# Inner fifth products in three more units of a gated feed-forward pass, with its sums placed anew

## The chip, the cores and the metric

The kernel runs on one core of a Trainium2 chip. The metric is the time of one execution on the device, in microseconds (us); lower is better.

## The reference

A pre-norm block of two parts, for 2048 tokens of width 1024, inputs and output in bfloat16:

```
h  = x + A(layernorm(x))       # linear attention: wqkv, 32 heads, phi(t) = (t+1 if t>0 else exp(t)) + 1e-6, wo
h2 = h + B(layernorm(h))
B(x) = (relu(x @ W_gate) * (x @ W_up)) @ W_down     # 1024 -> 3584 -> 1024
```

The change lies in B. It does not touch the attention part.

## The kernel before, in words

**Products by seven instead of eight.** A matrix product is cut into 2 x 2 blocks and done as seven block products P1 to P7 instead of eight (Strassen's scheme, in Winograd's form). It needs sums of blocks of the activations (`Ssum`, four arrays S1 to S4) and of the weights (`Tring`, four arrays T1 to T4 for each unit). The sums of the results are made partly in PSUM: a finished P1 is copied by ScalarE into the bank where the next product goes on adding (the forks `fk1`, `fk2`), and P5 is kept in SBUF (`s5`) and added at the evacuations c22 and c12.

**An inner step.** One of the block products can itself be done by seven smaller ones: 14 matmuls of 256 columns instead of 8 of 512. For P1 these are R1 to R7, done during the unit before (line 1725, `inner1`, says for which units). For P5 they are M1 to M7, at the start of the unit and between its other products (line 1722, `M0`, lists the units of pass 0; pass 1 does it in all). The inner P5 needs four sums xs of S1, once for a pass (`x_inner`, in `xs5`), and three instructions g5 for each unit on its T1 (`w_inner`, from T1 to `g5`); the sum `s5a` on VectorE takes the place of two copies by ScalarE, and small copies M5c, M1c, M6c and M4c come in. The inner P1 likewise needs three instructions g1 (`w_inner1`) on the raw weights and a sum Ra in PSUM.

**Two passes, units and a down pass.** The feed-forward part works on 1024 tokens at a time (pass 0 and pass 1). A pass has 14 units (`ffn_unit`, line 1728): even units compute the gate, with relu, odd ones the up projection, with the multiplication by the gate, both for the same four tiles of 128 of the 3584 columns; unit n uses ring slots of raw weights W (three units deep) and of T. The results `hh` stay in SBUF. Then the down pass multiplies them by W_down, again by seven products (pi = 0 to 6), most of which are themselves done by seven (`level2`: M1, M7, M6, M2, M5, M4, M3, each of 28 matmuls of 256 columns, with one weight load of 448 KB); in pass 0 products 0 and 2 are plain (`direct`: five chunks of weights). They use the four PSUM banks `XB` or `YB`. Loaded weights pass through a ring of 7 slots in pass 0 and 9 in pass 1, in the order of the list `WLIST`.

**Sums of sums.** The down pass needs sums of `hh`: D1 and D3 (`hh_pair`, two tiles at a time, done by VectorE in odd units), D2 and D4, and from them the inner sums sg3 to sg7. It also needs sums of W_down. VectorE makes those of the first level from raw weights (WT, `wd_pair`) in even units and of the second (WL, `wl_sums`) in odd ones; GpSimd makes some of the second level (WM and half of WL in pass 0; WY, `y_wsums`, in pass 1). All are stored in DRAM and loaded again in the down pass. A GpSimd sum waits for the matmul that was issued last when it was put into the program; its place in a unit is a call of `run(mid, n)`.

**LayerNorm of pass 1** (LN) is spread over the units of pass 0: for each of eight tiles a mean and a square on ScalarE, each followed by small steps of GpSimd on 128x1 (`_v`, `_v2`, `_r`, `lnn`), and a normalization. It goes to DRAM and comes back transposed (T5d, a DMA). Four of the tiles come back early into `hnE`, and ScalarE copies them (`hnc`, `early_c`) into `hnT`, when pass 0 no longer reads it. In this kernel `hnE` lies in RE, on the place of `xs5` and `g5`, so it is filled from unit 11 on.

**What sets the order.** The order of each engine's work is written out by hand. An instruction is appended to its engine's program when the Python code reaches it, and each engine, and the SP queue that issues most DMAs, runs its program in that order. In `ffn_unit` lists of further work are put into fixed places: `pre` at the start, `wina` after the first products, `winb` ahead of P7, then c22, `lnb` and `winc`, later c12 and `tail`, then P4. `lna` comes early in a unit without the inner P5 and after c22 in one of pass 0 with it. In the down pass `at(pi, ci, ...)` puts work behind part ci of product pi. Waits follow from `_Buf` objects: a reader waits for the last writer, a writer for all readers, and `over` or `claim` name other buffers on the same memory.

Almost all matmuls have line 904 in the profile, ScalarE's copies 909, most VectorE work of a unit 1776, and g1, g5 line 1688, T 1644 and 1649, D1 and D3 1665 and 1668, sg 1987, D2, D4 and the sums of the down pass 2051, WM 881, GpSimd's WL 871, WY 806.

Of the kernel before, what the change touches and what calls it, by code (L numbers as in the profile page):

```python
# [132 lines left out]
def bass_sequential_preLN__linear_attn_block__glu_gated_reglu__prompt_kernel(  # L133
# [71 lines left out]
    with es:  # L205
# [80 lines left out]
        hnE = RE[:, 4 * D:8 * D].rearrange("p (t a c) -> p t a c", t=STB, c=P)  # L286
# [52 lines left out]
        xn = RXH[:, 0:NXN * D].rearrange("p (a b) -> p a b", a=NXN)  # L339
        TWo_x = RXH[:, 0:KH * D].bitcast(f16).rearrange("p (j k c) -> p j k c", j=2, k=KH)  # L340
# [240 lines left out]
        for b_ in B_D1:  # L581
            b_.over = B_xn + B_TWo[0::2] + B_hs + hp_x
# [14 lines left out]
        for b_ in B_hnE:  # L597
            b_.over = B_o + B_oT[0:NOE]
        for b_ in B_hnE:
            b_.over = b_.over + B_xs5 + flat(B_g5)  # L600
        for b_ in B_xs5 + flat(B_g5):
            b_.over = B_o + B_oT[0:NOE]
        for b_ in B_V:
            b_.over = B_hnE
# [103 lines left out]
        ORDER = [list(range(7)), [0, 2, 1, 3, 4, 5, 6]]  # L708
# [952 lines left out]

        def hh_pair(q):
            f1, f2, f3 = 2 * q, 2 * q + 1, 2 * q + 4
            t0, t1 = slice(0, SBW), slice(SBW, 2 * SBW)
            PL.add("dve", lambda e: e.tensor_tensor(out=D1[:, q:q + 2, :], in0=hh[:, f1:f3:2, t1],
                                                    in1=hh[:, f2:f3:2, t1], op=ALU.add),
                   reads=[B_hh[f][1] for f in range(f1, f3)], writes=B_D1[q:q + 2], name="D1_%d" % q)
            PL.add("dve", lambda e: e.tensor_tensor(out=hh16[:, f1:f3:2, t1], in0=hh[:, f1:f3:2, t0],
                                                    in1=hh[:, f1:f3:2, t1], op=ALU.subtract),
                   reads=[B_hh[f][0] for f in (f1, f1 + 2)], writes=[B_hh[f][1] for f in (f1, f1 + 2)],  # L1670
                   name="D3_%d" % q)
# [56 lines left out]
        def ffn_unit(ps_, n, pre, wina, winb, mid=(), lna=(), lnb=(), tail=(), tail2=(), winc=()):  # L1728
# [211 lines left out]
            go(lnb)  # L1940
# [3 lines left out]
            go(winc)  # L1944
# [10 lines left out]
            evac5(1, 0, BC_, c12, B_c12, "c12")  # L1955
            go(tail)
# [76 lines left out]
        def down_pass(ps_, fill):  # L2033
# [128 lines left out]
            def d2(a, b):  # L2162
                tt(D2[:, a:b, :], D1[:, a:b, :], hh[:, 2 * a:2 * b:2, 0:SBW],
                   B_D1[a:b] + [B_hh[2 * q][0] for q in range(a, b)], [B_D2], "D2", op=ALU.subtract)

# [6 lines left out]
            def direct(pi, bk, act_ops, start, evac):  # L2172
                af, ab = act_ops
                for ci, (q0, q1) in enumerate(WCH):
                    def go(ci=ci, q0=q0, q1=q1):
                        ws = wd_slot(wd_use[0])
                        wd_use[0] += 1
                        w = wdring[ws]

                        def d_mm(q, j):  # L2180
                            mm(bank(bk[j]), af(q, j), w[:, (q - q0) * NW:(q - q0 + 1) * NW], start and q == 0,
                               q == NPAIR - 1, [ab(q), B_wd[ws]], B_bank[bk[j]], "d%d_%d_%d" % (pi, ps_, q), skip=True)

                        if q1 == NPAIR:
                            for j in range(STB):
                                for q in range(q0, q1):
                                    d_mm(q, j)
                            load_wd_next()
                            for j in range(STB):
                                evac(j)  # L2190
                        else:
                            for q in range(q0, q1):
                                for j in range(STB):
                                    d_mm(q, j)
                            load_wd_next()
                    units.append(((pi, ci), go))
# [89 lines left out]
            claim([B_D2], B_S)  # L2286
# [9 lines left out]
            for i in range(4):  # L2296
                at(1, 2 + i if not last else (2, 3, 4, 5)[i], sg7[i])
            if not last:
                at(0, 0, lambda: d2(0, NH), lambda: d2(NH, NPAIR))
                at(0, 1, sg6[0])  # L2300
                at(0, 2, *sg6[1:3])
                at(0, 3, sg6[3])
                for i in range(4):
                    at(2, 1 + i, sg5[i])
                claim(B_sgg, B_w[0:4])
                at(2, 2, lambda: d4(0, NH))
                for i in range(4):
                    at(2, 1 + i, sg4[i])
                at(3, 0, lambda: d4(NH, NPAIR))
            else:  # L2310
# [9 lines left out]
                at(0, 6, lambda: d2(0, NH))  # L2320
                at(2, 0, lambda: d2(NH, NPAIR))
# [330 lines left out]
        for p_ in range(NPASS):  # L2652
            done = []
            for q in range(NPAIR):
# [9 lines left out]
                if q > 1 and q % 2:  # L2664
                    wina.append(lambda q=q: hh_pair(q - 3))
                if p_ == 0:
                    raw, lna, lnb, tail = [], [], [], []
                    if q > 0 and ln_q:
                        for t in done:
                            early.append(t)  # L2670
                        f_, t0 = ln_q.pop(0)
                        lna.append(f_)
                        f_, t1 = ln_q.pop(0)
                        lnb.append(f_)
                        done = [t for t in (t0, t1) if t is not None and t < STB]
                    winc = []
                    for _ in range(2 if q == NPAIR - 1 else 1):
                        if q > 10 and early:
                            early_t(early.pop(0))
                    if q % 2 == 0:  # L2680
                        wds = wd_pair(q)
                        (tail if q == 0 else wina).extend(wds[0:2])
                        (tail if q == 0 or q in M0 else winb).append(wds[2])
                        wls, raw, nxt_raw, raw_l = wl_sums(q // 2)
                    else:
                        wina += wls
                        raw = raw_l
                        nxt_raw()
                        if q == NPAIR - 1:
                            for _ in range(4):  # L2690
# [11 lines left out]
                    ffn_unit(0, q, pre, wina, winb, raw, lna, lnb, tail, winc=winc)  # L2702
# [5 lines left out]
                if q == 0:  # L2708
# [6 lines left out]
                    wys = [f_ for m in range(NM) for f_ in y_wsums(m)]  # L2715
# [23 lines left out]
                if q == NPAIR - 1:  # L2739
# [3 lines left out]
                    for i in range(NWX):  # L2743
                        claim([B_wd[NWS + i]], [B_w[i]])
                        load_wd_next()
            for f_ in late21:
                f_()
            late21.clear()
            hh_pair(NPAIR - 2)
# [4 lines left out]
            else:  # L2754
                claim(B_V, B_xs5 + flat(B_g5))
# [4 lines left out]
            if p_ + 1 < NPASS:  # L2760
                late = [(lambda t=t: early_c(t), (0, t)) for t in range(STB)]
                late += [(lambda t=t: late_t(t), ((0, 1), (0, 3), (2, 0), (2, 1))[t - STB]) for t in range(STB, TPP)]
# [9 lines left out]
                late += [(nxt_s, (3, 1))] + [(ss[i], ((3, 3), (3, 5), (6, 0), (6, 2))[i]) for i in range(4)]  # L2772
# [71 lines left out]
```

## Time and profile before

| what | value |
|---|---|
| median of 3 runs | 710.98 us (710.78 to 712.07) |
| the profiled execution | 711.03 us |
| its span | 709.3 us |
| granted TensorE clock | 0.999 of full speed |
| units of pass 0 | 222.6 to 389.1 of the span |
| down pass of pass 0 | 389.1 to 466.8 |
| units of pass 1 | 466.8 to 631.0 |
| down pass of pass 1 | 631.0 to 706.4 |

The page counts an engine as busy while any of its instructions runs, so a pipelined TensorE appears nearly full; pauses are found from the starts of its matmuls and from the chain of work, which names the instruction that released each step. In a row of stretches, `11.69 (x69)` is the busy time and the number of instructions in it; the last three numbers are the granted clock, the DMA engines' busy share and GB/s. The digits of the 40 slices of the span, each 17.7 us, show where VectorE is full:

```profile
DVE  7988867899899899999998787887989888989996
ACT  4887666764863687778785411146666667651010
POOL 3221100114893334243522001321111110000331
```

### The profile page before, as it was taken

To read this page: it belongs to the slowest core of one execution; us is meant where nothing else is said; L and a number is where in the kernel's file an instruction comes from. 1 tells how busy PE (TensorE), PEld (TensorE's weight loads), DVE (VectorE), ACT (ScalarE), POOL (GpSimd) and SP (SyncE) were. 2 spreads that over 40 slices of the span, in tenths; PEclk is the share of its full clock that TensorE was granted. 3 is DMA by queue.
4 is the path that set the end of the run, shared out by engine and by line. 5 is a ranking of instruction groups with operands and counts; after the bars stand their busy time and mean duration, and the time that the engine had idled before them with its cause. 6 is when DMAs were issued, how large, how long until landed. Compare 5 with 4: busy or idle time off the path is not lost.

```text
span 709.3 us, 13488 instructions
## 1 busy us (share of the span) xinstructions
PE 704.0 (99%) x5101; PEld 398.3 (56%) x5101; DVE 612.4 (86%) x970; ACT 409.6 (58%) x743; POOL 179.5 (25%) x246
## 2 busy tenths in 40 slices
PE   9999999999999999999999999999999999999998
PEld 4444444444444455555554658865555555568887
DVE  7988867899899899999998787887989888989996
ACT  4887666764863687778785411146666667651010
POOL 3221100114893334243522001321111110000331
PEclk9999999999999999999999999999999999999999
DMA  9852244014999795968899999998465644268996
GB/s 304 255 123 61 39 133 161 29 31 97 231 208 285 233 345 170 304 215 252 271 292 290 310 243 320 315 243 239 133 190 156 193 147 125 87 236 312 345 283 184
DMA packets 170385, 148.80 MB, mean 210 GB/s; under 512 B 54352, under 2 KB 146896, under 8 KB 170320
## 3 DMA queue, kind: packets, MB, share of 16 engines
q1 hardware_dynamic: 165328, 143.35, 67.2%
q0 software_dynamic: 4032, 3.67, 3.5%
q8 instruction: 40, 0.66, 0.4%
q10 hardware_dynamic: 960, 0.92, 0.4%
q14 instruction: 25, 0.20, 0.1%
HBM read 101.97 MB, written 33.88 MB: 192 GB/s over the span
## 4 chain that ended last, share of the span: by engine, by line
PE 93%; DVE 3%; DMA 2%; issue 1%; SPq 0%; DVEq 0%
PE ps L904 93%; DMA RAB<-RXH 1%; DMA RE<-in_A_x_dram 1%; DVE RWG L1152 1%; DVE RC L1127 0%; SPq L655 0%; DVE RE L1776 0%; DVE RW L1127 0%; DVE st L918 0%; DVE RE L991 0%; DVE RXH L1029 0%; DVE RH L1152 0%; DVE RX L1247 0%; DVE RX L988 0%; DVE RE L1688 0%
## 5 line engine op out<-in xcount | busy, mean ns | idle before, releaser
L909 ACT ACTIVATE ps<-ps 128x512 f32<-128x512 f32 (+1 forms) x275 | 138.9, 515 | 181.9 <-PE ps L904 136.4
L904 PE MATMUL ps<-RC,RO 128*128 128x512 f16 (+1 forms) x600 | 141.8, 366 | 0.0
L904 PEld LDWEIGHTS ps<-RC,RO 128*128 128x128 f16 x600 | 58.4, 98 | 49.6 <-ACT ps L909 1.2
L909 ACT ACTIVATE RE<-ps 128x512 f32<-128x512 f32 (+3 forms) x106 | 63.8, 619 | 30.8 <-PE ps L904 12.8
L904 PE MATMUL ps<-RC,RWG 128*128 128x512 f16 x320 | 80.9, 379 | 0.2 <-ACT ps L909 0.2
L904 PE MATMUL ps<-RH,RWG 128*128 128x512 bf16 (+1 forms) x348 | 77.7, 348 | 0.0
L1776 DVE TENSOR_TENSOR RE<-ps,RE 128x1024 bf16<-128x1024 f32 (+1 forms) x46 | 46.6, 1013 | 25.7 <-PE ps L904 23.8
L904 PE MATMUL ps<-RH,RO 128*128 128x512 bf16 (+1 forms) x256 | 65.3, 379 | 0.0
L2060 POOL DMA_DIRECT2D out_dram<-RX x20 | 18.0, 1302 | 150.9 <-DMA RX<-out_dram 75.9
L904 PE MATMUL ps<-RW,RAB 128*128 128x256 f16 (+3 forms) x358 | 52.8, 300 | 0.0
L904 PEld LDWEIGHTS ps<-RH,RWG 128*128 128x128 bf16 x348 | 33.6, 98 | 34.1 <-ACT ps L909 0.3
L904 PE MATMUL ps<-RAB 128*128 128x512 bf16 (+3 forms) x242 | 51.1, 348 | 0.0
L904 PEld LDWEIGHTS ps<-RC,RWG 128*128 128x128 bf16 (+1 forms) x320 | 30.0, 98 | 33.8 <-ACT ps L909 5.1
L904 PEld LDWEIGHTS ps<-RW,RAB 128*128 128x128 f16 (+1 forms) x358 | 34.9, 98 | 14.1 <-DVE RXH L1482 0.5
L806 POOL TENSOR_TENSOR RW<-RW 128x256 f16<-128x256 bf16 x28 | 18.8, 672 | 90.1 <-PE ps L904 70.3
L2051 DVE TENSOR_TENSOR RE<-ps,RE 128x512 f32<-128x512 f32 x46 | 31.6, 686 | 11.3 <-PE ps L904 10.7
L1776 DVE TENSOR_TENSOR RAB<-RAB,RE 128x1024 bf16<-128x1024 bf16 (+1 forms) x43 | 37.4, 872 | 2.0 <-ACT RE L909 1.1
L1776 DVE TENSOR_TENSOR RAB<-ps,RE 128x1024 bf16<-128x1024 f32 x28 | 34.3, 1223 | 5.0 <-PE ps L904 4.7
L1788 ACT ACTIVATE RAB<-RAB 128x1024 bf16<-128x1024 bf16 x28 | 29.5, 1052 | 15.6 <-DVE RAB L1776 15.6
L904 PEld LDWEIGHTS ps<-RH,RO 128*128 128x128 f16 (+1 forms) x256 | 24.4, 98 | 24.6 <-ACT RX L909 1.5
L1644 DVE TENSOR_TENSOR RO<-RWG,RO 128x1024 f16<-128x1024 bf16 x54 | 37.9, 702 | 0.0
L909 ACT ACTIVATE RAB<-ps 128x512 bf16<-128x512 f32 (+2 forms) x54 | 35.6, 659 | 1.6 <-PE ps L904 1.6
(221 smaller groups left out, 1361.4 us busy)
## 6 DMA issues: line engine op xcount, KB each, us to landing
RWG<-in_B_W_gate_dram SPq DMA_DIRECT2D x28, 512.0 KB, 5.7
RWG<-in_B_W_up_dram SPq DMA_DIRECT2D x28, 512.0 KB, 5.3
RW<-l_scr SPq DMA_DIRECT2D x21, 448.0 KB, 5.4
RW<-in_B_W_down_dram SPq DMA_DIRECT2D x14, 512.0 KB, 6.1
l_scr<-RX SPq DMA_DIRECT2D x7, 1024.0 KB, 6.3
RE<-l_scr SPq DMA_DIRECT2D x16, 448.0 KB, 4.7
RW<-t_scr SPq DMA_DIRECT2D x13, 448.0 KB, 5.7
RE<-in_A_x_dram SPq DMA_DIRECT2D x19, 256.0 KB, 3.4
```

What stands on the lines that cost most here:

```text
L806: PL.add("pool", lambda e: e.tensor_tensor(out=ly[:, j, :], in0=x[0], in1=y[0], op=ALU.subtract), deps=[PL.prog["pe"][-1]], reads=x[1] + y ...
L904: lambda e: e.matmul(out_ap, lhsT, rhs, start=start, stop=stop, skip_group_check=skip),
L909: PL.add("act", lambda e: e.activation(out=dst, in_=src, func=func), reads=reads, writes=writes, name=name)
L1152: PL.add("dve", lambda e: e.tensor_tensor(out=s(i), in0=in0, in1=in1, op=op), reads=reads, writes=[B_Sx[i][p]], name="Sx%d_%d" % (i + 1, p))
L1644: PL.add(eng, lambda e: e.tensor_tensor(out=tb(j)[0](r), in0=x[0](r), in1=y[0](r), op=ALU.subtract), reads=rd, writes=bt(j, r), name="T%d_ ...
L1776: PL.add("dve", lambda e: e.tensor_tensor(out=dst, in0=in0, in1=in1, op=op), reads=reads, writes=writes, name=name)
L1788: PL.add("act", lambda e: e.activation(out=d, in_=d, func=ACTF.Relu), reads=[], writes=db, name=name)
L2051: PL.add(eng, lambda e: e.tensor_tensor(out=dst, in0=in0, in1=in1, op=op), reads=reads, writes=writes, name=name)
L2060: PL.add("pool", lambda e: e.dma_start(dst, src, accum_op=ALU.add), reads=[bsrc], writes=[B_hscr[st]], slot=sl, name="acc_%d_%d" % (st, dh))
```

## The change

It does these things:

- The inner P5 is used in units 2, 12 and 13 of pass 0 too, and the inner P1 for unit 2 (`M0`, `inner1`). For that the xs sums are made in unit 0, ahead of its P7, instead of at the end of unit 2, and g5 of the next unit comes first in `tail`. In inner even units WT's third sum moves from ahead of `tail` or within it to its end.
- `hnE` moves to RXH, on the place of D1 for tiles 6 to 13. The four transposes T5d go to units 8 to 11, and the copies `hnc` into the tail of unit 13, instead of the down pass.
- So D1 and D3 of tiles 6 to 13 are no longer made in units 9, 11, 13 and after, but in one instruction each in the down pass, and D2 in two pieces with them.
- In pass 0 the down pass takes its products in the order 0, 2, 1, 3, as pass 1 does. Product 1 then uses the banks XB. The first chunk of product 2 goes bank by bank. The sums sg, D4 and those of the next pass get other places.
- LN's `lnb` comes after c12, and so behind the GpSimd sum there, instead of after c22; unit 11 takes one step more.
- GpSimd's WM sums of unit 0 go in pairs after P7 and P3, and in pass 1 a filler (`int`) stands after each group of four WY sums.
- Two W_down loads move from ahead of unit 13 into unit 12.

`d1_sum(a, b)`, `d2_sum` and `d3_sum` are D1, D2 and D3 for the tiles a to b - 1, each in one VectorE instruction. The core of the diff, in the order of the file (ffn_unit, the down pass, the units of pass 0, pass 1, and what follows the units):

```diff
-        hnE = RE[:, 4 * D:8 * D].rearrange("p (t a c) -> p t a c", t=STB, c=P)
+        hnE = RXH[:, 3 * D:7 * D].rearrange("p (t a c) -> p t a c", t=STB, c=P)
...
-        ORDER = [list(range(7)), [0, 2, 1, 3, 4, 5, 6]]
+        ORDER = [[0, 2, 1, 3, 4, 5, 6]] * 2
...
+        def d1_sum(a, b):
+            PL.add("dve", lambda e: e.tensor_tensor(out=D1[:, a:b, :], in0=hh[:, 2 * a:2 * b:2, t1_],
+                                                    in1=hh[:, 2 * a + 1:2 * b:2, t1_], op=ALU.add),
...
+        def d3_sum(a, b):
...
+        def d2_sum(a, b):
...
         def hh_pair(q):
+            d1_sum(q, q + 2)
+            d3_sum(q, q + 2)
...
-        M0 = (4, 6, 8, 10)
-        NO_R = (0, 2)
+        M0 = (2, 4, 6, 8, 10, 12, 13)
+        QD = 6
+        LN3 = (11,)
         def inner1(ps_, n):
-            return 0 < n < NPAIR and (ps_, n) != NO_R
+            return 0 < n < NPAIR
...
             if m_first:
                 go(lna)
-            go(lnb)
...
             evac5(1, 0, BC_, c12, B_c12, "c12")
+            go(lnb)
             go(tail)
...
+                            jq = [(j, q) for j in range(STB) for q in range(q0, q1)]
+                            if start or ci:
+                                jq.sort(key=lambda x: x[1])
+                            for j, q in jq:
+                                d_mm(q, j)
...
                 direct(0, XB, a_hh(0, 0), True, e_s1)
-                level2(1, YB, q_d2, sgs[1], ev("dU", (U, U)))
                 direct(2, XB, a_hh(1, 0), False, e_11)
+                level2(1, XB, q_d2, sgs[1], ev("dU", (U, U)))
...
+                at(0, 4, lambda: d1_sum(QD, NPAIR), lambda: d2_sum(QD, NPAIR))
+                at(2, 0, *sg6[0:2])
+                at(2, 1, *sg6[2:4])
+                at(2, 2, lambda: d3_sum(QD, NPAIR), *sg7[0:2])
+                at(2, 3, *sg7[2:4])
+                at(2, 4, *sg4)
+                at(1, 1, lambda: d4(0, NH))
+                at(1, 5, lambda: d4(NH, NPAIR))
                 for i in range(4):
+                    at(3, 2 + i, sg5[i])
...
-                if q > 1 and q % 2:
+                if q > 1 and q % 2 and (p_ or q - 3 < QD):
                     wina.append(lambda q=q: hh_pair(q - 3))
...
+                    if q > 7 and early:
+                        early_t(early.pop(0))
...
+                        if q == 0:
+                            raw = [int, int] + [lambda i=i, r=raw: (r[i](), r[i + 1]()) for i in (0, 2)]
...
+                    if q == NPAIR - 1:
+                        tail += [lambda t=t: early_c(t) for t in range(STB)]
                     if q + 1 in M0:
-                        tail += w_inner(q + 1)
+                        tail = w_inner(q + 1) + tail
+                    if q and q % 2 == 0 and q in M0:
+                        tail.append(wds[2])
                     if q + 2 == min(M0):
-                        tail += x_inner()
+                        winb += x_inner()
...
-                    wys = [f_ for m in range(NM) for f_ in y_wsums(m)]
+                    wys = [f_ for m in range(NM) for f_ in y_wsums(m) + [int]]
...
+            if p_ == 0:
+                claim([B_D2], B_S)
+                d2_sum(0, QD)
```

More of the change, by code (lines that the diff above doesn't have):

```diff
@@ L581, in bass_sequential_preLN__linear_attn_block__glu_gated_reglu__prompt_kernel @@
         for b_ in B_D1:
-            b_.over = B_xn + B_TWo[0::2] + B_hs + hp_x
+            b_.over = B_xn + B_TWo[0::2] + B_hnE + B_hs + hp_x
         for b_ in B_Ef:
@@ L597, in bass_sequential_preLN__linear_attn_block__glu_gated_reglu__prompt_kernel @@
         for b_ in B_hnE:
-            b_.over = B_o + B_oT[0:NOE]
-        for b_ in B_hnE:
-            b_.over = b_.over + B_xs5 + flat(B_g5)
+            b_.over = B_xn + B_TWo[0::2] + B_hs + hp_x
         for b_ in B_xs5 + flat(B_g5):
@@ L603, in bass_sequential_preLN__linear_attn_block__glu_gated_reglu__prompt_kernel @@
         for b_ in B_V:
-            b_.over = B_hnE
+            b_.over = B_xs5 + flat(B_g5)
         for b_ in flat(B_hh) + B_out2:
@@ L1660, in t_sums @@
                     add(3, wb(1, 0), tb(1), 1))
-        def hh_pair(q):
[L1663 to L1671, printed above, removed]
+        t0_, t1_ = slice(0, SBW), slice(SBW, 2 * SBW)
+        def d1_sum(a, b):
+            PL.add("dve", lambda e: e.tensor_tensor(out=D1[:, a:b, :], in0=hh[:, 2 * a:2 * b:2, t1_],
+                                                    in1=hh[:, 2 * a + 1:2 * b:2, t1_], op=ALU.add),
+                   reads=[B_hh[f][1] for f in range(2 * a, 2 * b)], writes=B_D1[a:b], name="D1_%d" % a)
+        def d3_sum(a, b):
+            PL.add("dve", lambda e: e.tensor_tensor(out=hh16[:, 2 * a:2 * b:2, t1_], in0=hh[:, 2 * a:2 * b:2, t0_],
+                                                    in1=hh[:, 2 * a:2 * b:2, t1_], op=ALU.subtract),
+                   reads=[B_hh[f][0] for f in range(2 * a, 2 * b, 2)],
+                   writes=[B_hh[f][1] for f in range(2 * a, 2 * b, 2)], name="D3_%d" % a)
+        def d2_sum(a, b):
+            PL.add("dve", lambda e: e.tensor_tensor(out=D2[:, a:b, :], in0=D1[:, a:b, :], in1=hh[:, 2 * a:2 * b:2, t0_],
+                                                    op=ALU.subtract),
+                   reads=B_D1[a:b] + [B_hh[2 * q][0] for q in range(a, b)], writes=[B_D2], name="D2")
+        def hh_pair(q):
+            d1_sum(q, q + 2)
+            d3_sum(q, q + 2)
         def w_inner1(ps_, n):
@@ L1720, in bass_sequential_preLN__linear_attn_block__glu_gated_reglu__prompt_kernel, with ffn_unit @@
         late21 = []
-        M0 = (4, 6, 8, 10)
-        NO_R = (0, 2)
+        M0 = (2, 4, 6, 8, 10, 12, 13)
+        QD = 6
+        LN3 = (11,)
         def inner1(ps_, n):
-            return 0 < n < NPAIR and (ps_, n) != NO_R
-        def ffn_unit(ps_, n, pre, wina, winb, mid=(), lna=(), lnb=(), tail=(), tail2=(), winc=()):
+            return 0 < n < NPAIR
+        def ffn_unit(ps_, n, pre, wina, winb, mid=(), lna=(), lnb=(), tail=(), tail2=()):
             Lg = (ps_ * NPAIR + n) * 2
@@ L1943, in ffn_unit @@
                 dve(d, d, c12, B_c12, db, "h11", ALU.mult)
-            go(winc)
             if not up:
@@ L2160, in a_hh @@
                        (lambda q: B_hh[2 * q + k][t])
-            def d2(a, b):
-                tt(D2[:, a:b, :], D1[:, a:b, :], hh[:, 2 * a:2 * b:2, 0:SBW],
-                   B_D1[a:b] + [B_hh[2 * q][0] for q in range(a, b)], [B_D2], "D2", op=ALU.subtract)
             def d4(a, b):
@@ L2191, in go @@
                         else:
-                            for q in range(q0, q1):
-                                for j in range(STB):
-                                    d_mm(q, j)
+                            jq = [(j, q) for j in range(STB) for q in range(q0, q1)]
[3 more added lines that the diff above has]
+                                d_mm(q, j)
                             load_wd_next()
@@ L2284, in each @@
                 return [lambda j=j: f_(*args, j) for j in order]
-            claim([B_D2], B_S)
+            if last:
+                claim([B_D2], B_S)
             claim(U[1][2:4], B_c22 + B_c12)
@@ L2295, in down_pass @@
             sg5 = l2_sums(q_d1, sgs[4], "sg5")
-            for i in range(4):
-                at(1, 2 + i if not last else (2, 3, 4, 5)[i], sg7[i])
             if not last:
[L2299 to L2302, printed above, removed]
+                claim(B_sgg, B_w[0:4])
+                at(0, 4, lambda: d1_sum(QD, NPAIR), lambda: d2_sum(QD, NPAIR))
[6 more added lines that the diff above has]
+                at(1, 5, lambda: d4(NH, NPAIR))
                 for i in range(4):
-                    at(2, 1 + i, sg5[i])
-                claim(B_sgg, B_w[0:4])
-                at(2, 2, lambda: d4(0, NH))
+                    at(3, 2 + i, sg5[i])
+            else:
                 for i in range(4):
-                    at(2, 1 + i, sg4[i])
-                at(3, 0, lambda: d4(NH, NPAIR))
-            else:
+                    at(1, 2 + i, sg7[i])
                 claim(B_W, B_hnT)
@@ L2319, in down_pass @@
                 spread(0, sg2)
-                at(0, 6, lambda: d2(0, NH))
-                at(2, 0, lambda: d2(NH, NPAIR))
+                at(0, 6, lambda: d2_sum(0, NH))
+                at(2, 0, lambda: d2_sum(NH, NPAIR))
                 spread(2, sg6)
@@ L2672, in bass_sequential_preLN__linear_attn_block__glu_gated_reglu__prompt_kernel @@
                         lna.append(f_)
-                        f_, t1 = ln_q.pop(0)
-                        lnb.append(f_)
+                        t1 = None
+                        if ln_q:
+                            f_, t1 = ln_q.pop(0)
+                            lnb.append(f_)
                         done = [t for t in (t0, t1) if t is not None and t < STB]
[L2676 to L2679, printed above, removed]
+                        if q == NPAIR - 2:
+                            lna += [load_wd_next] * 2
+                        if q in LN3 and ln_q:
+                            f_, t0 = ln_q.pop(0)
+                            lnb.append(f_)
+                            done += [t for t in (t0,) if t is not None and t < STB]
+                    if q > 7 and early:
+                        early_t(early.pop(0))
                     if q % 2 == 0:
@@ L2682, in bass_sequential_preLN__linear_attn_block__glu_gated_reglu__prompt_kernel @@
                         (tail if q == 0 else wina).extend(wds[0:2])
-                        (tail if q == 0 or q in M0 else winb).append(wds[2])
+                        if q == 0 or q not in M0:
+                            (winb if q else tail).append(wds[2])
                         wls, raw, nxt_raw, raw_l = wl_sums(q // 2)
+                        if q == 0:
+                            raw = [int, int] + [lambda i=i, r=raw: (r[i](), r[i + 1]()) for i in (0, 2)]
                     else:
@@ L2689, in bass_sequential_preLN__linear_attn_block__glu_gated_reglu__prompt_kernel @@
                         if q == NPAIR - 1:
-                            for _ in range(4):
+                            for _ in range(2):
                                 load_wd_next()
@@ L2745, in bass_sequential_preLN__linear_attn_block__glu_gated_reglu__prompt_kernel @@
                         load_wd_next()
+            if p_ == 0:
+                claim([B_D2], B_S)
+                d2_sum(0, QD)
             for f_ in late21:
@@ L2748, in bass_sequential_preLN__linear_attn_block__glu_gated_reglu__prompt_kernel @@
             late21.clear()
-            hh_pair(NPAIR - 2)
             if p_ == 0:
@@ L2754, in bass_sequential_preLN__linear_attn_block__glu_gated_reglu__prompt_kernel @@
             else:
+                hh_pair(NPAIR - 2)
                 claim(B_V, B_xs5 + flat(B_g5))
@@ L2760, in bass_sequential_preLN__linear_attn_block__glu_gated_reglu__prompt_kernel @@
             if p_ + 1 < NPASS:
-                late = [(lambda t=t: early_c(t), (0, t)) for t in range(STB)]
-                late += [(lambda t=t: late_t(t), ((0, 1), (0, 3), (2, 0), (2, 1))[t - STB]) for t in range(STB, TPP)]
+                late = [(lambda t=t: late_t(t), ((0, 1), (0, 3), (2, 0), (2, 1))[t - STB]) for t in range(STB, TPP)]
                 def nxt_t():
@@ L2771, in bass_sequential_preLN__linear_attn_block__glu_gated_reglu__prompt_kernel @@
                 ts = t_sums((p_ + 1) * NPAIR * 2)
-                late += [(nxt_s, (3, 1))] + [(ss[i], ((3, 3), (3, 5), (6, 0), (6, 2))[i]) for i in range(4)]
+                late += [(nxt_s, (1, 5))] + [(ss[i], ((1, 6), (3, 1), (4, 6), (6, 2))[i]) for i in range(4)]
                 late += [(nxt_t, (5, 0))] + [(ts[i], (6, i)) for i in range(3)]
```

2 lines of the change are left out of this document (1 added, 1 removed).

## The prediction

> **What bounds the kernel now.** I read the page first, then the chain of work, then a table of stretches, one per unit, then the timelines around the few places where TensorE paused. The page gives TensorE the whole span and VectorE most of it:
>
> ```profile
> PE 704.0 (99%) x5101; PEld 398.3 (56%) x5101; DVE 612.4 (86%) x970; ACT 409.6 (58%) x743; POOL 179.5 (25%) x246
> ```
>
> The chain of work, in order of time (start, length, what), is TensorE from 42.90 to the end, left only where something was late:
>
> ```profile
> 42.90 272.47 PE ps L904 x2216
> ...
> 317.80 1.22 DVE RE L1776
> 319.02 0.74 DVE RE L1688
> 319.76 0.05 issue
> 319.80 172.87 PE ps L904 x1118
> 492.68 0.05 issue
> 492.72 190.57 PE ps L904 x1274
> ```
>
> So time is saved only by fewer TensorE columns or by removing a pause; VectorE, at 93 to 97% inside a unit, is the engine that can turn into a new bound. Next the stretches; each row is one unit of pass 0, in order units 1, 2, 4, 5, 8, 12, 13, and last unit 13 of pass 1 (bounds, length, then busy us of PE, PEld, DVE, ACT, POOL):
>
> ```profile
> 236.24:246.64 10.40, 10.40 (x50) 4.59 (x48) 9.22 (x12) 7.80 (x14) 3.11 (x6) 1.00 0.72 216
> 246.64:260.25 13.61, 13.61 (x71) 6.85 (x70) 12.33 (x16) 9.94 (x17) 5.37 (x6) 1.00 1.06 336
> ...
> 272.14:283.83 11.69, 11.69 (x69) 6.61 (x68) 11.10 (x19) 10.09 (x19) 4.52 (x7) 1.00 0.70 227
> 283.83:295.72 11.89, 11.89 (x63) 6.08 (x62) 10.90 (x17) 9.16 (x17) 2.72 (x3) 1.00 0.92 279
> 319.30:331.29 11.99, 11.87 (x69) 6.47 (x68) 11.49 (x19) 10.12 (x19) 4.11 (x6) 1.00 0.85 270
> 366.76:378.65 11.89, 11.89 (x64) 6.08 (x63) 11.52 (x16) 9.67 (x17) 6.45 (x7) 1.00 1.15 322
> 378.65:389.05 10.40, 10.40 (x49) 4.60 (x48) 7.54 (x10) 5.73 (x10) 0.00 (x0) 1.00 0.96 274
> 620.90:631.02 10.12, 10.12 (x55) 5.25 (x54) 8.02 (x13) 6.26 (x12) 0.00 (x0) 1.00 0.48 153
> ```
>
> The reader sees that a unit with the inner fifth product (4) is 0.20 shorter than one without (5), and that unit 8, of the same form as 4, is 0.30 too long.
>
> **Part 1, the columns.** P5 is 8 matmuls of 512 columns; its inner form is 14 of 256, 512 columns fewer, and so is the inner P1. Starts of matmuls in the trace lie 0.215 us apart at 512 and 0.108 at 256, so one such exchange gives 8 x 0.215 - 14 x 0.108 = 0.21. By whole units: unit 1 takes on the inner P1 of unit 2 and becomes like unit 5 (10.40 to 11.89, +1.49); unit 2 becomes like unit 4 (13.61 to 11.69, -1.92); unit 12 likewise (11.89 to 11.69, -0.20); unit 13 like unit 13 of pass 1 (starts 620.89 to 631.05: 10.40 to 10.16, -0.24). Sum **-0.87**, with 24 more matmuls (5125). The Trainium skill, "TensorE: Matmul & The Clock Gate", section "Back-to-back issue gap", gives for real streams of weight loads and matmuls 81 ns at 128 columns and 131 at 512. By a straight line, an estimate from that page, 256 columns would cost 98 ns and an exchange would lose 14 x 98 - 8 x 131, 0.32 us; four would add 1.3. The spacings above and units 4 and 5 decide against it, so it has no chance here.
>
> **Part 2, GpSimd's sums.** Unit 8 waited 0.29 for its inner weights: the first of the three sums g5 took 0.81 (0.42 in unit 5, at 295.36), beside one of GpSimd's sums (timeline of all engines: start, length, engine, line):
>
> ```profile
> 318.08 0.27 POOL L1583 TENSOR_SCALAR s<-s 128x1 f32<-128x1 f32 x1
> 318.31 1.16 POOL L871 TENSOR_TENSOR RX<-RW,RX 128x512 f16<-128x512 f16 x1
> ...
> 318.93 0.81 DVE L1688 TENSOR_TENSOR RE<-RO 128x512 f16<-128x512 f16 x1
> ...
> 319.80 0.11 PEld L904 LDWEIGHTS ps<-RE 128*128 128x128 f16 x2 [0.40 <-DVE RE L1688]
> ```
>
> That sum stood behind three LN steps, which waited for ScalarE. In unit 5 it ran 294.09 to 295.24, just ahead of g5. With the LN steps moved behind it, unit 7 looks like unit 5: **-0.30**. In pass 1 the filler entry after each group of four of GpSimd's sums does the same: at 489.11 a sum, released late by the store of the group before it, made h11 take 1.11 instead of 0.68:
>
> ```profile
> 489.11 0.67 POOL L806 TENSOR_TENSOR RW<-RW 128x256 f16<-128x256 bf16 x1 [4.00 <-DMA l_scr<-RW]
> 489.21 1.11 DVE L1776 TENSOR_TENSOR RAB<-RAB,RE 128x1024 bf16<-128x1024 bf16 x1
> ```
>
> Ra, c12 and the next fork came late, and units 1 and 2 of pass 1 lasted 11.86 and 11.91 instead of 11.69. With the filler that sum starts one place later, beside Ra and c12, which read PSUM; such rows keep their 0.69 and 1.22 beside a sum elsewhere (317.20, 315.46). **-0.39**. Bounds of part 2: 0 to -0.69.
>
> **Part 3, VectorE's added work, in units.** Each new inner unit adds three g5 sums (0.45 + 0.32 + 0.21 from start to start) and s5a (0.60); unit 1 adds three g1 sums (1.07) and Ra (0.60); a split T13 costs 0.1 in units 2 and 12. Pass 0 loses the pairs D1, D3 (1.33 each) of units 9, 11 and 13 to the down pass. The four xs sums (1.47) move from unit 2 to unit 0, and there they meet c22, which waited 0.92 for TensorE after a T13 of 1.69, stretched (1.22 elsewhere) by two of GpSimd's sums that move behind P7. T13 then ends at 230.95, the xs sums at 232.4, and c22 starts at 232.45 against 232.40: free; if T13 stays at 1.69, c22 ends at 234.15, with P4 due at 234.29. In unit 1, g1 to T13 end 7.6 after its start and c22 is due at 8.05. From there units 2, 12 and 13 run the order of units 4 and 6. Their closest meetings are T2 before P6 (0.16 spare), g5 before M5 (0.35) and Ra before R4 (0.3). I take 0; bounds -0.1 to +1.8 (six such places at 0.3 each, unit 8's size). ScalarE gains nine copies and in inner units is at 86%; it waits 0.46 ahead of fk1 in even units, and LN's step behind h22 uses that up. Its four hnc copies in unit 13 (4 x 0.94) delay h21c by some 0.7; behind it stand h21 and D1, due 20 us later. 0.
>
> **Part 4, the down pass.** TensorE does the same columns in the order 0, 2, 1, 3. Product 2 adds to the banks that product 0 leaves, so it waits for the four ds1 copies (400.10, 0.50 apart, last end 402.17); its first chunk goes bank by bank, 0.64 each, and each copy is 0.4 to 0.9 early: 0. VectorE gets D1, D2, D3 in pieces of up to 4096 elements (2.3 by the 3584 row's 2.02), then sg6, sg7, sg4, in all 19 us after h21 at 391; it is done near 410, product 1 starts at 412. sg7 overwrites what product 0 read, done by 400. In products 1 and 3 the closest is dV before M3, 0.4 spare. T5d moves earlier, to units 8 to 11, on SP ahead of that unit's loads; unit 11 carried one before without a pause, and weights land some 10 us ahead. 0, bounds -0.1 to +4 (below).
>
> **Sum.** -0.87 - 0.30 - 0.39 = -1.56. The profiled execution took 711.03 for a span of 709.27 (1.76 around it); 709.5 is the forecast for it and, its time being 0.05 over the median 710.98, for the median too (-0.2%). The measurement tells about 0.2%, 1.42 us, from no change: 709.56 to 712.40.
>
> **Rivals.**
> - *VectorE takes the place.* The spare of 0.16 at T2 is missed in the new inner units, or LN's small steps, now beside g5, hold g5 up as the sum in unit 7 did. The trace speaks against the second: LN's steps from 263.96 to 266.70 lay beside VectorE's WL and T4 sums, which kept 1.22 and 0.69, and it was the step that stretched (1.43 for 0.57). The Trainium skill, "SBUF — State Buffer", section "Who interferes with whom", says that a VectorE instruction with two SBUF inputs contends with a GpSimd one that reads SBUF, and that whichever issues first blocks the other; 318.93 and 489.21 bear it out, and by it a step that gets in ahead of g5 would stop it too. Price: three to six pauses of 0.3, so 710.4 to 711.3. Chance 0.20; no change.
> - *GpSimd's sums stay late* for another reason (a store, a load): only part 1 counts, 709.27 - 0.87 + 1.76, 710.2. Chance 0.12; no change.
> - *The weight loads fall behind*: slower. Product 1 moves behind 2, so five two-level products run in a row instead of four, each of their 35 small products lasting 1.53 and eating 448 KB from a ring of 7 slots. A slot comes round in 10.7; a load may take 9.2 from issue to landing. After the accumulating stores at 424 loads took 7.7 to 8.5, and the one issued at 427.22 landed at 435.69, 0.46 before its matmul. If they reach 10, TensorE loses 0.8 per turn, five turns, +4: 713.5; it decides from about 3 us of loss. Against it: the same stores now come after a calmer stretch, and the run of four recovered (margins of 2.3 and more one product later). Chance 0.08.
> - *More goes than counted*: the pauses of 0.08 to 0.16 in the down passes too, 709.0. Chance 0.04.
> - That the change doesn't do what it says is excluded: the lists of units fix the matmuls.
>
> **How the numbers follow.** The forecast, 0.56, reaches from 709.0 to 710.1, so 0.36 of it lies beyond 709.56 and 0.20 within. Faster 0.36 + 0.04 = 0.40; same 0.20 + 0.20 + 0.12 = 0.52; slower 0.08. The range 708.9 to 711.3 takes in all but the third rival and half of the rest's tails.
>
> **What would show it.** 5125 matmuls; unit 1 at 11.9, units 2, 8 and 12 at 11.7, 13 at 10.15; g5 of unit 8 at 0.42; units 1 and 2 of pass 1 at 11.7; no TensorE gap over 0.2 in products 1 and 3. Wrong if: a unit of pass 0 stays over these by 0.2 with T2 or g5 ending the wait (first rival), or weight slots end waits in the down pass (third).

## The result, and the profile after

The changed kernel takes 709.69 us (median of 19 runs, 709.05 to 710.38); the kernel before took 710.98 beside it (19 runs, 710.51 to 712.07). The ratio is 0.9982, with a 95% interval of 0.9974 to 0.9989: 0.8 to 1.85 us faster. The profiled execution took 709.65 for a span of 707.92.

The page, and then the chain of work (start, length, engine, line) of the kernel after:

```profile
PE 702.4 (99%) x5125; PEld 400.6 (57%) x5125; DVE 613.9 (87%) x982; ACT 412.5 (58%) x752; POOL 182.1 (26%) x246
```

```profile
207.52 474.52 PE ps L902 x3025
682.04 23.10 PE ps L902 x210
705.17 0.42 DVE RX L2060
```

There are 24 more matmuls and yet 1.6 us less TensorE time, and from 207.52 on the chain never leaves TensorE until the last evacuation: the place at 317.80 where it went over to VectorE is gone. The stretches, as in the prediction (units 1, 2, 8, 12, 13 of pass 0, unit 1 of pass 1):

```profile
236.51:248.41 11.90, 11.90 (x64) 6.08 (x63) 11.18 (x16) 9.08 (x18) 3.16 (x5) 1.00 0.72 218
248.41:260.10 11.69, 11.69 (x70) 6.59 (x69) 11.10 (x19) 10.20 (x20) 5.71 (x7) 1.00 0.90 290
...
319.15:330.84 11.69, 11.69 (x70) 6.59 (x69) 11.10 (x19) 10.20 (x20) 5.71 (x7) 1.00 1.03 309
366.29:377.98 11.69, 11.69 (x70) 6.60 (x69) 11.07 (x19) 9.16 (x18) 5.72 (x8) 1.00 0.90 302
377.98:388.14 10.16, 10.16 (x56) 5.28 (x55) 8.99 (x14) 8.78 (x15) 0.00 (x0) 1.00 0.77 224
...
479.38:491.07 11.69, 11.69 (x70) 6.64 (x69) 8.66 (x17) 7.54 (x16) 1.34 (x2) 1.00 0.86 250
```

Every unit has the length of its pattern. Two places in the timeline of VectorE and GpSimd show why. At the end of unit 7 GpSimd's sum is now done before g5 starts, and LN's steps come behind it; g5 takes 0.42 instead of 0.81:

```profile
317.47 1.16 POOL L869 TENSOR_TENSOR RX<-RW,RX 128x512 f16<-128x512 f16 x1 [1.01 <-PE ps L902]
317.60 1.22 DVE L1786 TENSOR_TENSOR RE<-ps,RE 128x1024 bf16<-128x1024 f32 x1
318.58 0.19 POOL L963 TENSOR_TENSOR s<-s 128x1 f32<-128x1 f32 x1
318.73 0.42 DVE L1697 TENSOR_TENSOR RE<-RO 128x512 f16<-128x512 f16 x1
```

In pass 1 the sum that held up h11 starts behind it, beside Ra and c12, which keep 0.69 and 1.22:

```profile
488.35 0.68 DVE L1786 TENSOR_TENSOR RAB<-RAB,RE 128x1024 bf16<-128x1024 bf16 x1
488.94 0.69 DVE L1786 TENSOR_TENSOR ps<-ps,RW 128x512 f32<-128x512 f32 x1
489.40 0.67 POOL L804 TENSOR_TENSOR RW<-RW 128x256 f16<-128x256 bf16 x1 [5.17 <-issue]
489.54 1.22 DVE L1786 TENSOR_TENSOR RE<-ps,RE 128x1024 bf16<-128x1024 f32 x1
```

Laid side by side by the starts of the matmuls, in us:

| stage | before | after | difference |
|---|---|---|---|
| start of unit 0 | 222.62 | 222.86 | +0.24 |
| units of pass 0 | 166.43 | 165.25 | -1.18 |
| down pass of pass 0 | 77.75 | 77.83 | +0.08 |
| units of pass 1 | 164.25 | 163.86 | -0.39 |
| down pass of pass 1 | 75.34 | 75.34 | 0 |

From unit 0 on the gain is 1.49. The attention part, whose code is the same, ended 0.24 later in this execution. Over all the profiles of this study unit 0 starts anywhere from 222.3 to 224.3, so below, effects are read from unit 0 on, in the one profiled execution of each kernel ("stages"), and the times stand beside them.

### The profile page after: what moved, and what is told of

Its sections match the earlier page's. It is cut to its first block, busy times and chain, and to the rows that moved or that the text cites. A ratio compares the mean times of both kernels' runs of the same rounds, so it can differ in the third digit from the quotient of the medians.

```text
span 707.9 us, 13556 instructions
## 1 busy us (share of the span) xinstructions
PE 702.4 (99%) x5125; PEld 400.6 (57%) x5125; DVE 613.9 (87%) x982; ACT 412.5 (58%) x752; POOL 182.1 (26%) x246
## 4 chain that ended last, share of the span: by engine, by line
PE 89%; ACT 2%; POOL 1%; DVE 1%; issue 1%; DMA 0%; DVEq 0%; POOLq 0%; SPq 0%; ACTq 0%
PE ps L902 89%; ACT RAB L942 1%; POOL RAB L1444 1%; DVE RXH L1526 1%; ACT RAB L1559 1%; DMA RE<-RE 0%; ACT RXH L942 0%; POOL s L966 0%; DVE RAB L989 0%; DVE rden L1384 0%; ACT ps L907 0%; POOL s L948 0%; POOL s L1543 0%; POOL s L963 0%; ACT RX L982 0%
## 5 line engine op out<-in xcount | busy, mean ns | idle before, releaser
L907 ACT ACTIVATE ps<-ps 128x512 f32<-128x512 f32 (+1 forms) x283 | 141.9, 511 | 184.0 <-PE ps L902 140.4
L902 PE MATMUL ps<-RC,RO 128*128 128x512 f16 (+1 forms) x588 | 138.5, 364 | 0.0
L1786 DVE TENSOR_TENSOR RE<-ps,RE 128x1024 bf16<-128x1024 f32 (+1 forms) x49 | 48.6, 993 | 27.4 <-PE ps L902 26.6
```

What stands on the lines that cost most here:

```text
L902: lambda e: e.matmul(out_ap, lhsT, rhs, start=start, stop=stop, skip_group_check=skip),
L907: PL.add("act", lambda e: e.activation(out=dst, in_=src, func=func), reads=reads, writes=writes, name=name)
L1786: PL.add("dve", lambda e: e.tensor_tensor(out=dst, in0=in0, in1=in1, op=op), reads=reads, writes=writes, name=name)
```

## The experiments

The theory: four exchanges of columns (-0.87), unit 8's pause (-0.30) and two pauses of pass 1 (-0.39) make the whole gain, and VectorE and the weight loads had just enough spare to add nothing. The rivals: one part's gain hides a loss of another, so that the parts alone add up otherwise; VectorE's spare was larger than read, so its risk was none; the same of the loads.

**The two new places of GpSimd's sums alone**, in the kernel before:

```diff
             if m_first:
                 go(lna)
-            go(lnb)
...
             evac5(1, 0, BC_, c12, B_c12, "c12")
+            go(lnb)
             go(tail)
...
-                    wys = [f_ for m in range(NM) for f_ in y_wsums(m)]
+                    wys = [f_ for m in range(NM) for f_ in y_wsums(m) + [int]]
```

> The kernel before with two edits alone: LN's second list goes behind the GpSimd sum at c12, and the filler stands after each group of four WY sums. Theory (the pauses come from GpSimd's sums meeting VectorE's, and go with this): unit 8 falls from 11.99 to 11.69, units 1 and 2 of pass 1 from 11.86 and 11.91 to 11.69, all others stay; span and time 0.69 less, 710.3 by the median, ratio 0.9990. Rival (the pauses have another cause, or came away by the new order of the other edits): these three units stay within 0.05 of before, time 711.0. Rival (LN's steps beside g5 stop VectorE): unit 8 is mended, but units 4, 6 or 10 grow by some 0.3 each.

Stages: -0.69 against before; unit 8 and units 1 and 2 of pass 1 last 11.69 each. Time 710.85, ratio 0.9997 (0.9988 to 1.0006), with the predicted 0.9990 inside; an effect of 0.69 is too small for the times to show. By the stages the part has its predicted size by itself.

**The new inner units undone**, all else as changed; xs comes in unit 2, still ahead of P7:

```diff
-        M0 = (2, 4, 6, 8, 10, 12, 13)
+        M0 = (4, 6, 8, 10)
+        NO_R = (0, 2)
...
-            return 0 < n < NPAIR
+            return 0 < n < NPAIR and (ps_, n) != NO_R
```

> The changed kernel with the inner P5 in units 4, 6, 8 and 10 alone and without the inner P1 of unit 2, as before; everything else as changed (places of the sums, hnE, the down pass). Theory (the columns are worth 0.87 and nothing of it was lost again): units 1, 2, 12 and 13 at 10.40, 13.61, 11.89 and 10.40, span 0.87 longer than the changed kernel's, time 710.5 by the median, ratio to before 0.9994. Rival (VectorE's work in the new inner units gives part of it back): the changed kernel gains less than 0.6 against this one, and units other than these four get shorter here. The down pass stays within 0.1 of the changed kernel's by both.

712.04, ratio 1.0013 (1.0004 to 1.0022), beyond the expected 0.9994. Stages: +1.66 over the changed kernel, 0.88 from the columns and 0.78 from something that was not expected, in unit 2. Its timeline:

```profile
254.61 1.71 POOL L879 TENSOR_TENSOR RAB<-RW 128x256 f16<-128x256 bf16 x1 [1.83 <-PE ps L902]
255.72 0.89 DVE L1718 TENSOR_TENSOR RE<-RC 128x512 f16<-128x512 f16 x1
...
256.78 0.81 POOL L879 TENSOR_TENSOR RAB<-RW,RAB 128x256 f16<-128x256 bf16 x1 [0.46 <-PE ps L902]
256.98 0.89 DVE L1718 TENSOR_TENSOR RE<-RC 128x512 f16<-128x512 f16 x1
...
259.40 0.82 PE L902 MATMUL ps<-RH,RO 128*128 128x512 bf16 x3 [0.61 <-DVE RAB L1787]
```

Two of the four xs sums ran beside GpSimd's WM sums and took 0.89 instead of 0.42; c22 came late, and P4 had to wait for it. In unit 0 of the changed kernel the WM sums stand behind P7, and nothing meets. So this run mixed two things; the next one parts them.

**The same, with xs at the end of unit 2**, as before the change:

```diff
-                        winb += x_inner()
+                        tail += x_inner()
```

> As the second run, but with the four xs sums at the end of unit 2, as in the kernel before, and not ahead of its P7, where two of GpSimd's sums doubled two of them (0.89 for 0.42) and c22 came late. Theory (the columns are worth 0.87, and the rest of the second run's loss was that meeting): units 1, 2, 12 and 13 at 10.40, 13.61, 11.89 and 10.40 without a pause, the span from unit 0 to the end 0.87 longer than the changed kernel's and 0.77 shorter than the second run's; ratio to before 0.9990. Rival (the units bring more than their columns): over 1.3 longer.

Stages: +0.87 over the changed kernel, no pause anywhere in the units. Time 711.28, ratio to before 1.0002 (0.9993 to 1.001), which leaves out the expected 0.9990; unit 0 started at 223.44 in its profile, 0.8 later than before. By the stages the columns are worth what the sum said; the times do not show it.

**LN's steps back behind c22**, in the changed kernel:

```diff
                 go(lna)
+            go(lnb)
...
             evac5(1, 0, BC_, c12, B_c12, "c12")
-            go(lnb)
```

> The changed kernel with LN's second list back behind c22, ahead of the GpSimd sum. Theory: the sum of unit 7 waits again for LN's steps and meets g5, so unit 8 lasts 11.9 to 12.0 instead of 11.69; unit 2, now an inner one with 0.16 to spare at T2, may lose up to 0.5 by the sum beside h2 in unit 1. Span 0.3 to 0.8 longer. Rival (the place of LN's steps does not matter): no unit moves by more than 0.05.

Stages: +1.33 (one run, 710.82), not the 0.30 that the same move is worth in the kernel before. Unit 8 loses 0.29 again, unit 2 the same 0.29, and unit 12 0.74, where three LN steps delay the sum:

```profile
366.75 1.45 DVE L1697 TENSOR_TENSOR RE<-RO,RE 128x256 f16<-128x256 f16 x2
366.81 1.25 POOL L869 TENSOR_TENSOR RX<-RW,RX 128x512 f16<-128x512 f16 x1
...
370.00 1.04 PE L902 MATMUL ps<-RC,RO 128*128 128x512 f16 x4 [0.57 <-DVE RO L1642]
```

Two small g5 sums took 1.45 instead of 0.62, T2 (line 1642) came late, and P6 waited. The new inner units and the new place of LN's steps depend on each other: with the old place the exchange would have brought 0.88 and cost 1.03 (1.33 less the 0.30 that unit 8 lost before).

**No filler in pass 1:**

```diff
-                    wys = [f_ for m in range(NM) for f_ in y_wsums(m) + [int]]
+                    wys = [f_ for m in range(NM) for f_ in y_wsums(m)]
```

> The changed kernel without the filler after each group of WY sums in pass 1. Theory: the first sum of the second group waits for the store of the first and starts beside h11 in unit 1 of pass 1; h11 takes 1.1, units 1 and 2 last 11.86 and 11.91, span 0.39 longer. Rival (that pause came from the beginning of pass 1, which the new down pass changes): units 1 and 2 of pass 1 stay at 11.69.

Stages: +0.23, of it 0.21 in unit 6 of pass 1 (one run, 709.96). Units 1 and 2 of pass 1 stayed at 11.69; the pause came there instead, by the same mechanism, a sum released by a store, beside h11:

```profile
534.91 0.67 POOL L804 TENSOR_TENSOR RW<-RW 128x256 f16<-128x256 bf16 x1 [3.85 <-DMA l_scr<-RW]
535.17 0.95 DVE L1786 TENSOR_TENSOR RAB<-RAB,RE 128x1024 bf16<-128x1024 bf16 x1
```

Where it strikes depends on when a store lands, so the 0.39 belongs to the profiled execution of before, not to the kernel for good: without the filler this one lost 0.21. The run of the kernel before with a smaller ring, below, has no filler either, and its units of pass 1 took 163.86 without any pause.

**g5 at the end of the tail:**

```diff
-                        tail = w_inner(q + 1) + tail
+                        tail += w_inner(q + 1)
```

> The changed kernel with the inner weight sums g5 behind T3 in the tail, which changes the order in unit 12 alone. Theory (M5 of unit 13 is 0.35 from its g5, and T3 takes 0.60): TensorE pauses 0.2 to 0.3 ahead of M5 in unit 13, which lasts 10.40 instead of 10.16; nothing else moves. Rival (the order within the tail does not matter): 10.16.

Stages: +0.26, all in unit 13 (10.42 for 10.16; one run, 709.33). There a T sum comes ahead of g5, and M5's weights wait for g5:

```profile
377.36 0.38 PE L902 MATMUL ps<-RC,RO 128*128 128x256 f16 x2
...
377.83 0.11 PEld L902 LDWEIGHTS ps<-RE 128*128 128x128 f16 x2 [0.37 <-DVE RE L1697]
377.83 0.39 PE L902 MATMUL ps<-RE 128*128 128x256 f16 x2
```

Between the starts of M1 and M5 lie 0.47, where two matmuls of 256 columns need 0.22.

**One more VectorE sum behind c12** in units 1, 3, 5, 7, 9 and 11, 128x1024 on a tile that nothing else uses (`extra`), to measure the spare of 0.16 at T2:

```diff
+                    if q % 2 and q < NPAIR - 1:
+                        tail.append(extra)
```

> The changed kernel with one more VectorE sum of 128x1024 in f16 (0.60 from start to start, on a tile of its own) at the end of the tail of units 1, 3, 5, 7, 9 and 11, ahead of h2 and T2. Theory (T2 before P6 has 0.16 to spare, whatever VectorE idles elsewhere): each of units 2, 4, 6, 8, 10 and 12 gets 0.44 longer, 2.6 in all, time 712.3. Rival (VectorE, busy 87% of the span and 12% idle in units 9 and 11, takes 3.6 us more in passing): under 0.1 each; or the units behind 9 and 11 are spared, and 1.8 in all.

713.14, ratio 1.0031 (1.0019 to 1.0044); stages +3.46. Units 2, 4, 6, 8 and 10 lose 0.51 to 0.53 each at P6:

```profile
250.75 0.69 DVE L1649 TENSOR_TENSOR RO<-RWG,RO 128x1024 f16<-128x1024 bf16 x1
...
251.50 1.04 PE L909 MATMUL ps<-RC,RO 128*128 128x512 f16 x4 [0.34 <-DVE RO L1649]
```

(the matmul starts show 0.50 between M2 and P6 here; the 0.34 is what is left of it after M2's modelled end). Unit 12 loses 0.76, as M5 waits 0.14 there too. The extra sum takes 0.60 from start to start, so the spare was about 0.09, not 0.16: T2 ends at 251.44 here and P6 starts at 251.50, and the 0.06 between them is missing in a spare that is counted up to T2's end. That, 0.08 in five units, with the 0.32 that unit 12 lost beyond the expected and 0.10 in unit 11, makes the surplus over 2.6.

**The same sum ahead of c22** (`winb.append(extra)`):

> The same additional sum in the same six units, but ahead of P7, where VectorE then waits 0.47 to 2.11 for the products of c22. Theory (it is the place that counts): hidden in units 3 to 11, at most 0.05 in units 1 and 2; under 0.1 in all, time 709.7. Rival (VectorE's total is what limits): as in the run with the sum after c12, some 2.6 more.

Stages: +0.04, in unit 6; no wait shows. Time 710.13, ratio 0.9988 (0.9978 to 0.9998), unit 0 starting 0.5 late. Six sums of 0.60 are free in one place and cost 3.46 in another, some 4.5 us later in the same program.

**Two more sums in units 9, 11 and 13**, in the place of the pairs D1 and D3 that went to the down pass:

```diff
+                    if q in (9, 11, 13):
+                        wina[:0] = [extra, extra]
```

> The changed kernel with two more VectorE sums of 128x1024 (the size of one pair D1, D3, on a tile of their own) in units 9, 11 and 13, where the kernel before makes such pairs. Theory: units 9 and 11, where VectorE waits 2.1 ahead of c22, stay at 11.89; in unit 13, where it waits 0.19, c22 comes 1.2 later and P4, due 0.24 behind its end, waits some 0.9: unit 13 lasts 11.0 instead of 10.16. Rival (the work moved to the down pass was needed for the new inner units 10 and 12): these grow by 0.3 or more. Rival (it was not needed at all): no unit moves.

712.51 (one run; 1.40 of that is unit 0's later start, at 224.26). Units 9 and 11 keep their length. Unit 13 lasts 11.58 instead of 10.16 and so loses 1.42, in one wait, P4 for c22 (one of P4's eight matmuls has no record in this trace, so the 1.47 is no exact measure of it):

```profile
389.42 0.81 PE L909 MATMUL ps<-RH,RO 128*128 128x512 bf16 x3 [1.47 <-DVE RE L1793]
```

I had expected 0.9. In the kernel after VectorE has 0.77 idle in unit 13, ahead of an evacuation at 382.12. Here the first extra sum took the place ahead of it and the second, with WL's sum of 1.22, came behind it, so that 1.30 stayed idle and c22 came 1.59 late, counted from the start of the unit, more than the 1.20 of the two sums. What the pairs would cost depends on their order among the other sums; that unit 13 has little room for them holds.

**A ring of 6 slots instead of 7** in pass 0, in the kernel after and in the one before:

```diff
-        RING = [[NWS - 2, NWS - 1] + list(range(NWS - 2)),
+        RING = [[NWS - 2, NWS - 1] + list(range(NWS - 3)),
```

(with one load fewer issued at the end of the units)

> The changed kernel with 6 slots instead of 7 for the weights of pass 0's down pass. A slot then comes round in 9.2, and a load may take 7.7; the longest in the changed kernel's trace takes 7.2, 1.75 ahead of its matmul. Theory (the order 0, 2, 1, 3 leaves more room, not less): no pause over 0.3 in products 1 and 3, span at most 0.3 longer. Rival (five two-level products in a row are close to the limit of the loads): pauses of 1 or more in products 1, 3 and 4.

> The kernel before with 6 slots in the same ring. Its tightest load landed 0.46 ahead of its matmul, in product 4. Theory: with 1.53 less, TensorE pauses about 1 in product 4, and more in all than the changed kernel does with 6 slots. Rival (the order of the products does not matter to the loads): both lose the same, within 0.2.

709.38 and 710.54 (one run each; the kernel before took 710.57 beside them). By the stages the changed kernel loses nothing. The kernel before takes 0.11 more in this down pass; from unit 0 to the end it is still 0.28 shorter than with 7 slots, as the pause of 0.39 in pass 1 did not come. This is the one wait on a weight load in its down pass:

```profile
434.50 0.99 PEld L904 LDWEIGHTS ps<-RE,RXH 128*128 128x128 f16 x10 [0.22 <-DMA RE<-t_scr]
```

My expectation for the old order, a loss of about 1, fell, and the rival's "the same, within 0.2" came true. The loads there landed sooner with one slot fewer: the longest after the stores took 7.46 us, and 8.46 with 7 slots. In the changed kernel the longest behind its stores fell likewise, from 7.18 to 6.33, but its longest of all, for product 6, took 7.28 with 6 slots and 7.26 with 7, and the smallest time between a landing and the matmul that needs it fell from 1.66 to 0.12. With 6 slots both orders are close to the limit, and the old one is just past it.

## Why the prediction was right

709.5 was predicted, 709.69 came.

- *Columns, -0.87*: -0.88, unit by unit (11.89, 11.69, 11.69 and 10.16 from start to start), and +0.87 when undone alone. The rule of the Trainium skill, "TensorE: Matmul & The Clock Gate", "Back-to-back issue gap", by which, in the prediction's estimate, the exchanges would lose 1.3, does not hold here: they gained 0.22 each.
- *GpSimd's sums, -0.30 and -0.39*: -0.30 and -0.39 by the stages, and -0.69 alone. One row was misread on the way: at 317.20, named for a sum that keeps its 0.69, only LN steps run beside it; the row at 488.94 of the kernel after shows it. The step left out how much more hung on it: in the changed kernel LN's new place is worth 1.33. The rival that these sums stay late did not come. The pass 1 share is the less lasting one, as it moves with the landing of a store: it was 0.39, 0.21 and 0 in the three profiles without the filler, so that it counted in full is partly luck.
- *VectorE, 0*: 0. The first rival named the right place, T2 before P6, and the spare there is even smaller than read (0.09); but the new inner units have the order of the old ones, and the change puts nothing between c12 and T2. The xs sums in unit 0 ran as worked out, c22 starting at 232.64. That they are free only because the WM sums were moved behind P7 was part of the working, and the run with xs in unit 2 shows the price, 0.78. "93 to 97%" read VectorE too full: in the rows shown it is busy 89 to 97% of units 1 to 12.
- *Down pass, 0*: +0.08. Product 4 lasts 10.86 instead of 10.78: M3 starts 0.16 late behind M4 instead of 0.08. In pass 1, which takes the products in the order 0, 2, 1, 3 in both kernels, the same pause is 0.17 before and after, so it seems to go with that order; why stays open. A variant with M5's result copied out of its bank, which was to take this pause away, gave no result. VectorE was done with the sums at 411.7, not near 410, with product 1 starting at 412.3. The slower rival did not come: with the order 0, 2, 1, 3 the longest load took 7.3 us and the smallest margin before a matmul was 1.66 us instead of 0.46. That a whole slot less cost nothing does not make it groundless, since only 0.12 of margin was left then. (Each of the seven small products of a product is 14 matmuls of 256 columns, not 28; the 1.53 of the prediction fits 14.)
- *From the span to the time*: 1.73 lay around the span, 1.76 was predicted. The 0.24 by which the attention part ended later was in no term. With it the 1.49 of the stages becomes 1.25, beside the 1.29 of the medians. That it was so small is luck, as the run with the units undone and xs late shows. By the stages it is 0.72 shorter than the kernel before, yet its median came out 0.27 above, and even the fastest of its 11 runs, 710.64, lies above the 710.29 that the stages would give. So up to 1 us outside these stages, most likely ahead of unit 0, belongs to that kernel and not to one execution, though the attention part's code is the same (0.6 if most executions of the kernel before lack the pause of 0.39 in pass 1). In the profiles the programs part first at the loads of the input: the fourth landed at 11.71 before, at 12.21 in the kernel after and at 12.26 with xs late. The cause stays open.

709.69 lies within the 1.42 us that the prediction took as too little to tell from no change. The 19 runs of each kernel tell more: the interval of 0.8 to 1.85 us leaves out no change.

## What to carry to other kernels

Price a sum by its place, not by its engine's share: find the next instruction that another engine waits for, and the idle time ahead of it. The same 0.6 us of VectorE work was free ahead of an evacuation that waits for TensorE, and cost 0.5 a unit behind the next one. And when two edits of one change each look small, ask what the first is worth once the second is in: LN's place was worth 0.30 alone and 1.33 with the new inner units.

## What the runs showed of the hardware

Where a GpSimd sum on 128x512 or 128x256 and a VectorE sum with two SBUF inputs met, one of them took longer. In the rows shown it was mostly VectorE: 0.62 became 1.45, 0.42 became 0.89, 0.68 became 0.95, with GpSimd at 1.25, 0.81 and 0.67 against 1.16, 0.67 and 0.67 alone. It could also be GpSimd: in the run with xs in unit 2 its sum at 254.61, begun 0.03 behind a VectorE sum (254.58, a T sum), took 1.71 instead of 0.67, and that VectorE sum kept its 1.22. Beside the same sums VectorE's reads of PSUM kept 0.69 and 1.22. The Trainium skill, "SBUF — State Buffer", section "Who interferes with whom", says that a VectorE instruction with two SBUF inputs and a GpSimd one that reads SBUF shut each other out, whichever issues first going first; these rows agree. GpSimd's steps on 128x1, which by that rule could stop g5 as well, did not: beside g5 in the kernel after they stretched themselves (0.73 instead of 0.57 at 318.85) and left it at 0.42 and 0.62.
